# Narrower stationary operands and a reordered chunk loop in an RWKV-7 kernel with a gated projection

## The chip, the cores and the metric

The kernel runs on one core of one Trainium2 chip. The metric is the device time of one execution in microseconds (us), and a kernel's time is the median of several executions. Nearly all runs of this study fell in the fast state (on one core this only means that a run did not stand over 1.5% above the fastest of its kernel). The exceptions are two of the four runs of e6_shift and six of the 113 runs of before that were made beside the experiments. Ratios use fast runs alone. Every run's output matched the reference.

Five engines work side by side (in before's profile the busy shares of four of them, 86, 58, 42 and 22%, add up to more than the span): TensorE (matmuls are "PE" in the profile, loads of the stationary operand "PEld"), VectorE (DVE), ScalarE (ACT), GpSimd (POOL) and SyncE (SP). "PEclk" is what the profile gives as the share of the full clock that was granted to TensorE.

## The reference

```python
# r, k, v, w, a, b: [4 batches, 8 heads, 768 steps, 40]
for t in range(S):                       # state: [4, 8, 40, 40]
    y[:, :, t] = einsum('bhd,bhde->bhe', r_t, state)
    Sa = einsum('bhde,bhe->bhd', state, a_t)
    state = state * w_t - einsum('bhd,bhe->bhde', Sa, b_t) \
          + einsum('bhd,bhe->bhde', v_t, k_t)
x = y as (3072, 320)                     # the bridge
h = x @ w_in                             # (3072, 2048)
out = (h * cos(h)) @ w_out               # (3072, 320)
```

## The kernel before

The recurrence is solved in 24 chunks of 32 steps. Each chunk is a list of *pieces* of TensorE work, with their evictions. The narrow pieces belong to the recurrence. Their operands occupy only 32 to 64 rows and columns, and several matmuls run on the array at a time: in before's trace eight of x start per 62.5 ns, about what 72 columns alone take at the 216 ns for 256 columns of a wide piece. Between them stand transposes. The wide pieces, `M` in the lists below, are a quarter of a step of the two dense products `x @ w_in` and `(h cos h) @ w_out` for tokens that are already done. They fill the time in which the recurrence waits for evictions.

| name in the list | tile in the profile | what it does | TensorE records |
|---|---|---|---|
| t | sT | state transposed | 16 |
| q | qps | r times state | 128 |
| x | x0ps | right-hand side of the triangular system | 256 |
| s | sps | its solution | 128 |
| z | dps | state update and output | 256 |
| g | gram | products of k, a, v, r of the next chunk | 256 |
| v, k, pw, pa, pb | vT, kT, wT, wn, bT | transposes | 8 to 16 |
| pn | nps | matrix for the inverse | 256 |
| M | ph or po | one quarter of a dense product | 16, some 32 |

A *record* is a load or a matmul as the trace has it. Each fp32 `matmul` call leaves two of both, so the 64 calls of z are 128 loads and 128 matmuls.

```python
    def ch_q(c):
        ps = at("qps")
        for i in range(2 * B):
            for e in range(2):
                for f in range(2):
                    mm(ps[full[e], f, i * C : (i + 1) * C], G["s"][half[f], i, full[e]],   # 64 columns
                       G["rT", c][half[f], 2 * (i % 2) + e, blk[i // 2]], i == 0)
        nc.scalar.copy(...)                       # one eviction of 128 rows into qz
    ...
    def first_b(g, j):
        first_full(g, j, 1)                       # 8 matmuls of 128 rows
        ...                                       # then the tails: 8 matmuls of 64 rows
    ...
        for c in range(NCH):
            ...
            elif c % 4 == 0 and q0 < NCH:
                segs = [t, M, v, q, M, k, x, M, g, M, s, M, pb, z, M, pn, M, M]
            elif c % 4 == 1 and q0 < NCH:
                segs = [t, M, v, q, M, k, x, M, pw, M, s, g, M, z, M, pa, M, pa1, M]
            elif c % 4 == 2 and q0 < NCH:
                segs = [t, M, pb, q, M, pn, M, x, v, M, s, k, M, z, M, g, M, M]
            elif c % 4 == 3 and q0 + 4 < NCH:
                segs = [t, M, pw, q, M, v, x, M, k, M, s, g, M, z, M, pa, M, pa1, M]
            else:
                segs = [t, M, v, M, q, M, k, x, M, g, M, s, M, z, M, M]
```

(Laid out more tightly than in the source, and cut. In most chunks a wide piece stands between two long narrow ones. That turns out to matter.)

## Time and profile before

| | before |
|---|---|
| median device time, first three runs | 875.13 us (872.48 to 877.44) |
| profiled execution | 869.9 us, mean granted clock 0.929 |
| TensorE matmuls / loads busy | 86% / 67% |
| VectorE / ScalarE busy | 58% / 42% |

The prediction below shows and reads the main lines. One line of the same page it does not show, and did not look at: among the DMA queues stands `q8 instruction: 130, 2.13, 1.0%`. These are 130 packets of 2.13 MB together, so 16,384 bytes each, that took 1.0% of the span of 16 DMA engines. By the profile's name for it the queue delivers instructions, not data. With its small share of the DMA engines' time it looks harmless.

### The profile page before, as it was taken

How to read it: one execution, taken by the hardware profiler on the slowest of the kernel's cores; microseconds unless marked ns; L12 is line 12 of the kernel's file. 1: busy time of each engine (PE TensorE's matmuls, PEld its weight loads, DVE VectorE, ACT ScalarE, POOL GpSimd, SP SyncE). 2: the span in 40 equal slices, each digit the busy share in tenths (PEclk: the TensorE clock that was granted, in tenths of full speed). 3: DMA queues.
4: the chain of work that ended last, by engine and by line, in shares of the span. 5: the costliest groups of instructions: out<-in, count | busy, mean ns of one | idle time of the engine just before them, and what ended most of it. 6: DMA issues, size and time to landing. Idle time of an engine off the chain costs nothing.

```text
span 869.9 us, 36861 instructions
## 1 busy us (share of the span) xinstructions
PE 751.9 (86%) x16472; PEld 585.0 (67%) x16472; DVE 505.5 (58%) x1074; ACT 364.5 (42%) x683; POOL 195.6 (22%) x342
## 2 busy tenths in 40 slices
PE   3535463998888997989999999999999999999997
PEld 3423352676666775777777777777777777777775
DVE  7788787349635597425578435588335775323322
ACT  0316555333234432534443453444435443534343
POOL 4306534120202132012132013203102221111000
PEclk9855567898999999999999999999999999999999
DMA  7456352412140420430420422313312202201000
GB/s 97 108 91 190 109 157 57 78 27 42 32 72 17 73 58 10 71 66 12 74 62 24 71 54 41 72 35 57 69 23 41 55 20 44 41 20 35 19 15 16
DMA packets 181854, 49.07 MB, mean 56 GB/s; under 512 B 156992, under 2 KB 178496, under 8 KB 181696
## 3 DMA queue, kind: packets, MB, share of 16 engines
q1 hardware_dynamic: 179264, 46.05, 25.4%
q8 instruction: 130, 2.13, 1.0%
q10 hardware_dynamic: 2176, 0.33, 0.3%
q0 software_dynamic: 256, 0.33, 0.2%
q14 instruction: 28, 0.23, 0.1%
HBM read 38.80 MB, written 7.86 MB: 54 GB/s over the span
## 4 chain that ended last, share of the span: by engine, by line
PE 63%; DVE 22%; ACT 7%; issue 4%; DMA 2%; POOL 0%; SPq 0%; DVEq 0%; ACTq 0%
PE ph L101 24%; PE po L101 17%; DVE inv L409 4%; PE dps L101 4%; DVE inv_tmp L405 4%; PE x0ps L101 3%; PE qps L101 2%; DVE rw L352 2%; PE gram L101 2%; PE sT L495 2%; DVE turns L649 2%; DVE wb L331 2%; PE nps L101 1%; ACT turns L654 1%; PE sps L101 1%
## 5 line engine op out<-in xcount | busy, mean ns | idle before, releaser
L101 PE MATMUL po<-w_out_sb,gT 128*128 128x320 f32 x768 | 228.2, 444 | 0.0
L101 PE MATMUL ph<-xT,w_in_sb 128*128 128x256 f32 x768 | 195.4, 401 | 11.0 <-DVE gT L657 8.0
L101 PEld LDWEIGHTS po<-w_out_sb,gT 128*128 128x128 f32 x768 | 141.4, 193 | 54.3 <-issue 4.8
L101 PEld LDWEIGHTS ph<-xT,w_in_sb 128*128 128x128 f32 x768 | 145.3, 198 | 33.9 <-issue 11.6
L649 DVE SCALAR_TENSOR_TENSOR turns<-turns,ph 128x512 f32<-128x512 f32 x96 | 61.7, 684 | 149.9 <-ACT turns L647 149.9
L647 ACT ACTIVATE turns<-ph,rnd 128x512 f32<-128x512 f32 x96 | 60.8, 684 | 199.6 <-PE ph L101 199.6
L586 POOL TENSOR_TENSOR qz<-qz,wc 128x160 f32<-128x160 f32 x92 | 42.8, 483 | 268.2 <-DVE qz L585 267.6
L657 DVE TENSOR_TENSOR gT<-ph,turns 128x512 f32<-128x512 f32 x96 | 65.4, 686 | 39.8 <-ACT turns L654 39.6
L409 DVE TENSOR_TENSOR inv<-inv,inv_tmp 128x31 f32<-128x31 f32 (+15 forms) x186 | 68.4, 368 | 6.4
L654 ACT ACTIVATE turns<-turns,half_pi 128x512 f32<-128x512 f32 x96 | 69.4, 722 | 3.1
L405 DVE TENSOR_TENSOR inv_tmp<-u,inv 128x31 f32<-128x31 f32 (+15 forms) x186 | 67.4, 362 | 4.2
L653 ACT ACTIVATE turns<-turns 128x512 f32<-128x512 f32 x96 | 60.3, 628 | 17.2 <-DVE turns L649 17.2
L585 DVE TENSOR_TENSOR qz<-dps,qz 128x160 f32<-128x160 f32 x92 | 29.2, 318 | 50.7 <-PE dps L101 50.7
L101 PE MATMUL ph<-xT,w_in_tail 64*128 64x256 f32 x384 | 54.4, 402 | 0.0
L352 DVE RECIPROCAL rw<-wn 128x320 f32<-128x320 f32 x24 | 51.6, 2151 | 3.3 <-PE wn L290 3.0
L101 PEld LDWEIGHTS ph<-xT,w_in_tail 64*128 64x128 f32 x384 | 33.1, 186 | 18.1 <-issue 15.7
L101 PE MATMUL dps<-vvm,kn 32*64 32x72 f32 x1536 | 28.5, 248 | 18.9 <-DVE sm L558 8.8
L101 PEld LDWEIGHTS dps<-vvm,kn 32*64 32x64 f32 x1536 | 22.7, 139 | 28.8 <-issue 15.1
L499 ACT COPY s<-sT 128x512 f32<-128x512 f32 x46 | 24.5, 585 | 36.3 <-PE sT L495 36.3
L333 POOL COPY wc<-wb 128x16 f32<-128x16 f32 x24 | 5.7, 237 | 137.6 <-DVE wb L331 137.6
L597 POOL TENSOR_TENSOR yt<-yt,wb 128x512 f32<-128x512 f32 x24 | 31.6, 1315 | 22.1 <-DVE yt L592 22.1
L536 DVE COPY x<-x0ps 128x288 f32<-128x288 f32 x24 | 10.8, 452 | 43.0 <-ACT x L535 43.0
(108 smaller groups left out, 1040.6 us busy)
## 6 DMA issues: line engine op xcount, KB each, us to landing
words<-in_moe_w_in_dram SPq DMA_DIRECT2D x8, 512.0 KB
nat_k<-in_k_dram SPq DMA_DIRECT2D x96, 40.0 KB
nat_v<-in_v_dram SPq DMA_DIRECT2D x96, 40.0 KB
nat_r<-in_r_dram SPq DMA_DIRECT2D x96, 40.0 KB
xd<-yt SPq DMA_DIRECT2D x48, 80.0 KB
out_dram<-ot SPq DMA_DIRECT2D x24, 160.0 KB
nat_w<-in_w_dram SPq DMA_DIRECT2D x88, 40.0 KB
nat_b<-in_b_dram SPq DMA_DIRECT2D x88, 40.0 KB
```

Of the source, the lines that this page charges most:

```text
L101: nc.tensor.matmul(o, lhsT=lhsT, rhs=rhs, start=start, stop=stop, skip_group_check=True)
L352: nc.vector.reciprocal(rw, unpad(wn.rearrange("p (h d) -> p h d", h=H)))
L405: nc.vector.tensor_tensor(tmp, u[:, j : j + 1, :j].to_broadcast([P, C - j, j]), x[:, j:, j : j + 1].to_broadcast([P, C - j, j]), ALU.mult,)
L409: nc.vector.tensor_tensor(x[:, j:, :j], x[:, j:, :j], tmp, ALU.subtract)
L585: nc.vector.tensor_tensor(z, pick(dp, 0, (2 * N72 + C, 2), (N72, 2), (1, D)), z, ALU.add)
L586: nc.gpsimd.tensor_tensor(z, z, wc.rearrange("p (f m b) -> p f m b", f=2, m=2)[:, :, :, bb] .unsqueeze(3).to_broadcast([P, 2, 2, D]), ALU. ...
L597: nc.gpsimd.tensor_tensor(yt.rearrange("p j b t -> p (j b) t"), yt.rearrange("p j b t -> p (j b) t"), wx, ALU.mult)
L647: nc.scalar.activation(n, u, ACTF.Identity, bias=rnd, scale=1.0)
L649: nc.vector.scalar_tensor_tensor(n, n, -ROUND, u, ALU.add, ALU.subtract)
L653: nc.scalar.activation(n, n, ACTF.Abs)
L654: nc.scalar.activation(n, n, ACTF.Sin, bias=half_pi, scale=-2.0 * math.pi)
L657: nc.vector.tensor_tensor(gT[:, 2 * e : 2 * e + 2].rearrange("p f t -> p (f t)"), us[e], ns[e], ALU.mult)
```

## The change

The intent is to spend less TensorE time on loads and on changes of the array's shape:

1. q, and the half of z that uses `bn`, load only the 40 columns that carry data, in place of 64. The price is a second eviction for q.
2. Pieces of one array shape are put next to each other: gram (g) directly behind x, and in every fourth chunk x directly behind pn, with x's state part first.
3. The 64-row "tails" of the first dense product come first when the piece ahead of them was narrow, so that the array goes from narrow to 64 rows to 128 rows.

```diff
-                        ps[full[e], f, i * C : (i + 1) * C], G["s"][half[f], i, full[e]],
+                        ps[half[e], f, i * C : (i + 1) * C], G["s"][half[f], i, half[e]],
 ...
+        for rows in half:
+            nc.scalar.copy(pick(qz[rows], ...), ps[rows, ...])
 ...                                             # ch_z, bn half
-                            n[blk[bb], 2 * j + e, :],
+                            n[blk[bb], 2 * j + e, : rows[e].stop - rows[e].start],
 ...                                             # first_b
+        if G["small"]:
+            tails(True)
+            first_full(g, j, 1, False)
+        else:
+            first_full(g, j, 1)
+            tails(False)
 ...                                             # c % 4 == 0, 1, 2, 3, and the last chunks
-                segs = [t, M, v, q, M, k, x, M, g, M, s, M, pb, z, M, pn, M, M]
+                segs = [t, M, v, q, M, k, x, g, M, s, M, pb, M, z, M, pn, M, M]
-                segs = [t, M, v, q, M, k, x, M, pw, M, s, g, M, z, M, pa, M, pa1, M]
+                segs = [t, M, v, q, M, k, x, g, M, pw, M, s, M, z, M, pa, M, pa1, M]
-                segs = [t, M, pb, q, M, pn, M, x, v, M, s, k, M, z, M, g, M, M]
+                segs = [t, M, pb, q, M, pn, x, M, v, M, s, k, M, z, M, g, M, M]
-                segs = [t, M, pw, q, M, v, x, M, k, M, s, g, M, z, M, pa, M, pa1, M]
+                segs = [t, M, pw, q, M, v, M, k, x, g, M, s, M, z, M, pa, M, pa1, M]
-                segs = [t, M, v, M, q, M, k, x, M, g, M, s, M, z, M, M]
+                segs = [t, M, v, q, M, k, x, g, M, s, M, M, z, M, M, M]
```

(Cut: the plumbing of `small` and of x's two parts, and c=4, which changes in the same way.)

More of the change, by code (lines that the diff above doesn't have):

```diff
@@ L304, in later, with step @@
         waiting.append([steps, work])
-    def step(work, of_inv=0, of_w=0):
+    def step(work, of_inv=0, of_w=0, small=False):
         before = list(waiting)
         work()
+        G["small"] = small
         for w in before:
@@ L506, in ch_q, with ch_x, of_a, of_state @@
                     mm(
-                        ps[full[e], f, i * C : (i + 1) * C], G["s"][half[f], i, full[e]],
+                        ps[half[e], f, i * C : (i + 1) * C], G["s"][half[f], i, half[e]],
                         G["rT", c][half[f], 2 * (i % 2) + e, blk[i // 2]], i == 0,
                     )
-        nc.scalar.copy(
-            pick(qz, 0, (NZ - C, 2), (NZ, 2 * B), (1, C)),
-            ps[:, :, : 2 * B * C].rearrange("p f (i t) -> p f i t", t=C),
-        )
-    def ch_x(c):
-        ps = at("x0ps")
-        for j in range(4):
-            o = C * (j // 2)
-            for bb in range(B):
-                for e in range(2):
-                    mm(
-                        ps[blk[bb ^ e], e, j * N72 : (j + 1) * N72], G["ag", c][blk[bb], 4 * e + j, :],
-                        vvm[c % 2][blk[bb], 2 * j + e, o : o + N72], j == 0,
-                    )
-        if c:
+        for rows in half:
+            nc.scalar.copy(
+                pick(qz[rows], 0, (NZ - C, 2), (NZ, 2 * B), (1, C)),
+                ps[rows, :, : 2 * B * C].rearrange("p f (i t) -> p f i t", t=C),
+            )
+    def ch_x(c, state_first=False):
+        ps = at("x0ps")
+        def of_a(first):
+            for j in range(4):
+                o = C * (j // 2)
+                for bb in range(B):
+                    for e in range(2):
+                        mm(
+                            ps[blk[bb ^ e], e, j * N72 : (j + 1) * N72],
+                            G["ag", c][blk[bb], 4 * e + j, :],
+                            vvm[c % 2][blk[bb], 2 * j + e, o : o + N72], first and j == 0,
+                        )
+        def of_state(first):
             for j in range(4):
@@ L531, in ch_x @@
                             ps[blk[bb ^ e], e, j * N72 : (j + 1) * N72],
-                            G["aT", c][half[e], j, blk[bb]], qz[half[e], bb, j % 2, o : o + N72], False,
-                        )
+                            G["aT", c][half[e], j, blk[bb]],
+                            qz[half[e], bb, j % 2, o : o + N72], first and j == 0,
+                        )
+        parts = [of_a] if c == 0 else [of_state, of_a] if state_first else [of_a, of_state]
+        for i, part in enumerate(parts):
+            part(i == 0)
         x0 = [sb1.tile([P, 4 * N72], F32, tag=f"x0{e}", name=f"x0{e}") for e in range(2)]
@@ L568, in ch_z @@
         for s, n in ((0, kn_b[c % 2]), (1, bn_b[c % 7])):
+            rows = half if s else full
             for j in range(4):
@@ L573, in ch_z @@
                         mm(
-                            ps[bb // 2][full[e], bb % 2, j * N72 : (j + 1) * N72],
-                            n[blk[bb], 2 * j + e, :],
+                            ps[bb // 2][rows[e], bb % 2, j * N72 : (j + 1) * N72],
+                            n[blk[bb], 2 * j + e, : rows[e].stop - rows[e].start],
                             sm[e][blk[bb], j, :] if s else vvm[c % 2][blk[bb], 2 * j + e, o : o + N72],
@@ L628, in first_a, with first_full @@
         first_full(g, j, 0)
-    def first_full(g, j, e):
+    def first_full(g, j, e, fresh=True):
         xT, ph = G["xT", g], G["ph"][e]
@@ L634, in first_full, with tails @@
                 cs = slice((4 * j + 2 * e + f) * P, (4 * j + 2 * e + f + 1) * P)
-                mm(ph[:, f, :], w_in_sb[:, i, cs], xT[:, i, :], i == 0 and f == 0, False)
+                mm(ph[:, f, :], w_in_sb[:, i, cs], xT[:, i, :], fresh and i == 0 and f == 0, False)
     def first_b(g, j):
-        first_full(g, j, 1)
         xT, phs = G["xT", g], G["ph"]
-        for f in range(2):
-            for e in range(2):
-                mm(phs[e][:, f, :], w_in_tail[full[e], j, f, :], xT[full[e], 2, :], False)
+        def tails(fresh):
+            for f in range(2):
+                for e in range(2):
+                    mm(
+                        phs[e][:, f, :], w_in_tail[full[e], j, f, :], xT[full[e], 2, :],
+                        fresh and e == 1 and f == 0, False,
+                    )
+        if G["small"]:
[4 more added lines that the diff above has]
+            tails(False)
         us = [ph.rearrange("p f t -> p (f t)") for ph in phs]
@@ L726, in last @@
                 later(1, lambda: p2_kn(c + 2))
-        return [lambda: ch_t(c), lambda: ch_q(c), lambda: ch_x(c), lambda: ch_s(c), last]
+        return [lambda: ch_t(c), lambda: ch_q(c), lambda: ch_x(c, c == 5 or c > 5 and c % 4 == 2), lambda: ch_s(c), last]
     with tc.manual_schedule():
@@ L814 @@
                 pw, pa, pa1, *p8 = p1(8)
-                segs = [t, M, v, q, M, k, x, M, g, M, s, M, z, M, pw, M, pa, pa1, M]
+                segs = [t, M, v, q, M, k, x, g, M, s, M, M, z, M, pw, M, pa, pa1, M]
                 fill = (3, 0)
@@ L849 @@
                 if seg is not M:
-                    step(seg, *fill)
+                    step(seg, *fill, small=seg in (q, x, g, s, z, pn))
                 elif empty > 0:
```

## The prediction

> **What bounds the kernel now.** I first read the page: busy shares, the 40 slices and the chain that ended last.
>
> ```profile
> PE 751.9 (86%) x16472; PEld 585.0 (67%) x16472; DVE 505.5 (58%) x1074; ACT 364.5 (42%) x683; POOL 195.6 (22%) x342
> ...
> PE   3535463998888997989999999999999999999997
> DVE  7788787349635597425578435588335775323322
> ...
> PEclk9855567898999999999999999999999999999999
> ...
> PE 63%; DVE 22%; ACT 7%; issue 4%; DMA 2%; POOL 0%; SPq 0%; DVEq 0%; ACTq 0%
> ```
>
> Up to about 225 us, and again from 313 to 338 us, the chain runs through VectorE (inv, inv_tmp: the triangular inverse). From chunk c=8 (352 us) to the end TensorE is nearly always busy at full clock, so a TensorE nanosecond saved there is one off the span. "Busy" is no measure of useful streaming, though. So I next read the timeline of TensorE for one stretch (c=13) and took the differences of the start times, first column:
>
> ```profile
> 511.35 1.14 PE L101 MATMUL qps<-rT,s 40*64 40x32 f32 x64
> 512.41 1.99 PE L101 MATMUL ph<-xT,w_in_sb 128*128 128x256 f32 x8
> 514.33 1.13 PE L101 MATMUL ph<-xT,w_in_tail 64*128 64x256 f32 x8
> 515.40 0.66 PE L290 MATMUL kT<-ident,kn 128*128 128x128 f32 x4
> 515.99 0.88 PE L101 MATMUL x0ps<-vvm,ag 32*32 32x72 f32 x64
> 516.80 0.89 PE L101 MATMUL x0ps<-qz,aT 40*32 40x72 f32 x64
> 517.61 2.42 PE L101 MATMUL po<-w_out_sb,gT 128*128 128x320 f32 x8
> 519.87 1.04 PE L290 MATMUL wT<-ident,nat_w 128*128 128x128 f32 x8
> ```
>
> Here q takes 1.06 us, the full products of the second half 1.92, the tails 1.07, kT 0.59, x 1.62 (two parts), po 2.26. Where the shape before and after is the same, the same work is shorter: eight full ph records take 1.73 us (216 ns each, as at 508.65), eight po 2.16, four transposes 0.44. Thus each change of array shape costs two things. The last record of the old shape stands 93 ns longer (309 ns to the next start in place of 216; 203 in place of 109 after transposes). And the first load of the new shape lies bare: po 2.26 less 2.16 is 0.10 us, about as much for ph and tail, 0.055 for a transpose, and I take 0.055 for a 64-column and 0.03 for a 32-column load.
>
> Inside q, starts of single records come in fours (the four 64x64 tiles), a period of 58 ns. Loads of one tile lie 55 ns apart at the start; streaming 32 columns twice takes only 27 ns (at 216 ns for 256 columns). So q waits for its loads. In z the same 64-column load hides: its period is 62.5 ns for eight tiles, just the 72 columns, and later in the stream 66 ns for eight, whatever the load's width (x and nps with 32 columns do the same).
>
> [...]
>
> **The change part by part.**
>
> *q, 40 columns.* [...] The period becomes about 38, and sixteen periods save 16 x 20 = 0.31 us with the ends. All 23 q calls get it, but only those outside the VectorE-bound stretches count: c=5, 6, 8 to 23, 18 calls, 18 x 0.31 = 5.6 us. The price is a second eviction of q: the row of qz<-qps shows 586 ns per copy of 128 rows; I assume that one of 40 rows takes as long, as the columns are the same, so ACT gets 23 x 0.59 = 13.5 us more. ACT is 42% busy and x comes 3 us later; I put nothing.
>
> *z, 40 columns for bn.* That load is hidden by streaming and by issue, so little: 0.5 us in all.
>
> *Fewer shape changes.* I wrote down the order of pieces per chunk before and after, by the loop's own rules. Tails first after a narrow piece: "q, full, tail, full" becomes "q, tail, full", one change fewer, 0.15 to 0.2 us. Gram directly behind x: x's second part and gram have both 40 rows and 32 columns, so "x, po, gram" loses two changes, 0.2 + 0.12 = 0.32 us. For c mod 4 = 2, x behind pn with the state part first saves the change between them. Counting all: 340 changes become 291, with 2 or 3 fewer per chunk, and 7.1 us for c from 4 on; without c=4 and 7, where VectorE rules, 6.7 us.
>
> *Waits that go.* For c = 8, 12, 16 z follows bT and waits for its eviction, as both PSUM buffers of the pool are needed. The chain of waits at c=12:
>
> ```profile
> 495.56 0.89 PE bT L290 x8
> 496.45 0.02 issue
> 496.48 1.08 ACT bT L366 x2
> 497.56 0.04 issue
> 497.60 1.63 PE dps L101 x87
> ```
>
> The changed order puts a product between: 3 x 1.1 = 3.3 us. For c = 9, 11, 13, 15, 17, 19 gram stands one product before z and its buffer is still being read by VectorE: z takes 1.77, 2.09, 2.09, 2.40, 2.06, 2.13 in place of 1.57, together 3.1 us; the new order frees it earlier. Likewise s to gram at c = 9, 13, 17 (waiting for the scan of pw), 0.27 each, 0.8.
>
> *A wait that comes.* Gram needs the eviction of kT. With k, x, gram in a row, only x (1.5 us) hides it. At c=13 the ACT timeline shows how late kT is:
>
> ```profile
> 515.50 1.27 ACT L647 ACTIVATE turns<-ph,rnd 128x512 f32<-128x512 f32 x2 [2.37 <-PE ph L101]
> 516.94 0.63 ACT L653 ACTIVATE turns<-turns 128x512 f32<-128x512 f32 x1 [0.18 <-DVE turns L649]
> 517.60 0.72 ACT L654 ACTIVATE turns<-turns,half_pi 128x512 f32<-128x512 f32 x1
> 518.23 0.57 ACT L458 COPY kT<-kT 128x512 f32<-128x512 f32 x1
> ```
>
> The products end at 515.40, kT is out at 518.80, 3.4 us later. Tails first complete the first half's PSUM 1.8 us earlier, so one rounding (0.68) moves out of this row and VectorE's part is done in time: kT at 2.7 us. TensorE arrives at 0.53 + 1.53 = 2.06. So gram waits about 0.66 us where k follows the products directly, c = 8, 9, 12, 13, 16, 17: 4.0 us lost. In the other chunks another product lies between. At c=19 "v, q, k" without a product costs about 1 us for buffers.
>
> Sum: 5.6 + 0.5 + 6.7 + 3.3 + 3.1 + 0.8 - 4.0 - 1.0 = 15.0 us. 875.1 - 15.0 = 860.
>
> **The rivals.** (a) Loads and streams of one tile run one after the other, not side by side: 27 + 27 + gaps also gives 58 ns. Then 40 columns save 10, not 20 ns, q gives 2.8 us, and the time is 863. Against it: nps (32-column loads, 32-column streams) starts in periods of 28 to 32 ns, which leaves no room for both in turn. (b) The kT wait is worse: if the rounding does not move forward (a wait on all of TensorE's earlier work, not on the first half), each wait is 1.3 us, -4 more, 864; with gram's arrival delaying x0 and s behind it, 867. For it: the ACT timeline above, where kT stands behind all of that row. (c) The kernel's rhythm is set by VectorE/ACT in more chunks than I think, so saved TensorE time comes back as waits: then half of 15, 867. Against it: from 414 to 690 us VectorE is busy 164 of 275 us, and TensorE 269. (d) Better: c=4 to 7, where TensorE idles some 15 us, gains from the new order too, and kT does not wait; 853.
>
> **How the range follows.** The counted parts (q, changes) are well founded; 12 us. The waits, +7 and -5, are each uncertain by half. TensorE also has stalls with no visible cause, 1.2 to 2.2 us each, about five after 250 us, which can move by some us, and the runs before spread by 5 us. So 853 to 868. Two per cent is 857.6, a little under my centre: faster 0.37, same 0.60, slower 0.03.
>
> **What would show it.** q's load row at 40 columns and q's start-to-next-start 0.75 us (0.90 if rival a). Gram behind x without the 93 ns step; tails 64*128 directly behind qps and dps. Chunks of about 30.5 us near 29. A wait gram <- ACT kT of about 4 us after 352 us (8 with rival b), and the waits dps <- ACT bT and dps <- DVE vvm gone. Wrong if q stays above 1 us, if shape changes cost the same after the reorder [...], or if new waits on ACT exceed 8 us.

The period of 38 ns for q is the prediction's estimate. It can be had from the trace of before, where the first two loads of one tile start 55 ns apart at 64 columns (q) and 108 at 128 (tails): 40/64 of 55 is 34 ns, 21 less, and 58 - 21 is 37. The 0.03 us that it takes for a 32-column load are, in the same way, half of the 55 ns. The 27 ns for streaming are 32/256 of the 216 that a record of 256 columns takes; that a load takes 27 ns too is rival (a)'s assumption.

## The result, and the profile after

The changed kernel took **913.48 us** (median of 4 runs, 909.94 to 916.62). The kernel before took 876.29 us (872.48 to 878.26, 4 runs) beside it. The ratio is 1.0429, 95% interval 1.0374 to 1.0483: slower, and far outside the predicted range of 853 to 868. A ratio in this document is the mean time of one kernel's fast runs over the mean time of the other's in the same rounds, so it is not quite the ratio of the medians quoted.

From the page of the changed kernel come the busy shares, the slices of TensorE and of its clock, the instruction queue, and the chain that ended last:

```profile
PE 762.4 (84%) x16472; PEld 591.3 (65%) x16472; DVE 508.0 (56%) x1074; ACT 378.2 (42%) x706; POOL 196.4 (22%) x342
...
PE   4525464888978879899999899989999899989997
...
PEclk9755576999989889999999989989999999999999
...
q8 instruction: 130, 2.13, 1.0%
...
PE 66%; DVE 17%; ACT 7%; issue 7%; DMA 2%; SPq 0%; POOL 0%; ACTq 0%; DVEq 0%
```

The work is the same, 16,472 matmuls, and yet their busy time grew from 751.9 to 762.4 us, although q's loads became narrower. "issue", time in which TensorE waits for nothing that the profile knows, went from 4 to 7% of the span. In the clock's row new dips to 8 stand in the middle, where before every slice from the eleventh on showed a 9.

The windows from c=8 to the end, first of before, then of after, put a size on it (columns: window, its length, busy us and count of PE, PEld, DVE, ACT, POOL, then granted clock, DMA share, GB/s):

```profile
352.40:864.30 511.90, 503.21 (x10764) 390.61 (x10763) 259.13 (x575) 226.89 (x425) 92.80 (x168) 1.00 0.21 43
```

```profile
361.80:905.40 543.60, 512.15 (x10765) 396.26 (x10763) 261.17 (x575) 236.56 (x441) 93.66 (x168) 0.96 0.21 40
```

This stretch became 31.7 us longer. TensorE's idle time in it (length less PE busy) rose from 8.7 to 31.5 us, and the clock fell from 1.00 to 0.96. No other engine has noticeably more to do, except the 16 more q copies of ACT, and in after all of them are less than half busy.

The view of waits, of the same stretch, for TensorE's loads, names what the loads waited for (us in total, times, longest); before, then after:

```profile
PEld gram L101 <- issue: 6.2, 15, 1.4
PEld dps L101 <- ACT bT L366: 3.1, 3, 1.0
...
PEld po L101 <- issue: 2.0, 6, 0.3
```

```profile
PEld gram L101 <- issue: 19.0, 14, 2.4
PEld po L101 <- issue: 13.7, 41, 2.3
...
PEld gram L101 <- ACT kT L459: 4.3, 8, 0.7
```

The wait for bT went, as predicted, and the wait for kT came, at its predicted size. But gram's waits for "issue" tripled, and single ones are 2.4 us long. So the timeline of TensorE for c=13, the same stretch as the prediction shows of before (columns: start, length, engine, line, out<-in, shape, elements, count, and in brackets the idle time ahead):

```profile
531.44 0.81 PE L101 MATMUL qps<-rT,s 40*40 40x32 f32 x64
532.18 1.13 PE L101 MATMUL ph<-xT,w_in_tail 64*128 64x256 f32 x8
533.25 1.99 PE L101 MATMUL ph<-xT,w_in_sb 128*128 128x256 f32 x8
535.08 0.60 PE L290 MATMUL kT<-ident,kn 128*128 128x128 f32 x4
535.61 0.88 PE L101 MATMUL x0ps<-vvm,ag 32*32 32x72 f32 x64
536.42 0.88 PE L101 MATMUL x0ps<-qz,aT 40*32 40x72 f32 x64
537.77 0.72 PE L101 MATMUL gram<-aT,kT 40*32 40x32 f32 x61 [0.46 <-ACT kT L459]
...
538.33 0.73 PE L101 MATMUL gram<-rT,vT 40*32 40x32 f32 x62
540.50 3.63 PE L101 MATMUL po<-w_out_sb,gT 128*128 128x320 f32 x8 [1.44 <-issue]
543.97 0.71 PE L290 MATMUL wT<-ident,nat_w 128*128 128x128 f32 x5
```

Differences of the first column: q 0.74 us, tails 1.07, the full products behind them 1.83. All these are gains, of the sizes predicted. Then two new things. Behind gram TensorE stops: po starts 2.17 us after gram's second half did, where 62 such records take 0.7 us, and the profile names no releaser. And po then takes 3.47 us in place of 2.26, since the trace's clock records show half clock from 539.78 to 543.19 us, a stretch of 3.41.

### What the stops have in common

I next listed, from the trace, the gaps between TensorE records (from the start of one to the start of the next), with the number of records executed by then, and the packets of the instruction queue. This number counts, besides loads and matmuls, the semaphore instructions of TensorE's sequencer, which the profile's pages leave out (344, and 3 drains, in after): without them the regularity below does not show, so I take it that they are fetched too. Six of after's gaps, and three of before's:

```text
start us  gap us  records/256  between                    packet start+us  restart after landing
after
 252.62    2.30      30.75     x0ps -> x0ps               252.4+1.24        1.29
 404.49    1.72      53.75     gram -> gram               403.6+1.24        1.36
 436.65    1.96      58.75     x0ps -> x0ps               436.3+1.07        1.21
 538.98    1.51      75.75     po load -> po matmul       537.9+1.02        1.55
 606.89    2.13      86.75     gram -> gram               606.4+1.33        1.30
 814.76    2.49     122.75     gram -> gram               814.7+1.35        1.24
before
 253.06    2.41      30.75     x0ps -> x0ps               252.6+1.32        1.54
 439.45    1.48      61.75     gram -> gram               438.6+0.93        1.43
 371.91    1.10      48.81     dps -> dps (wait for bT)   366.5+1.00        5.50
```

A gap with a known releaser, the last row, stands at another count (48.81 here, and 70.64 and 92.46 where before waits for bT again). The others in the list, which the profile calls "issue", all stand where the number of records is a whole number and three quarters of 256, and end 1.2 to 1.6 us after a packet of the instruction queue has landed. (Not every "issue" is of this kind: a few of 0.5 to 1.3 us stand elsewhere, such as one of 1.14 us at 28.08 in after, 2.5 us after a landing.) After's 33,291 records are 130.04 times 256, for 130 packets; a packet of 16,384 bytes for 256 records is 64 bytes a record. I read this so: TensorE gets its instructions in blocks of 256, and at these points it had run out of them. In the rows above that cost 1.5 to 2.5 us each time.

A block's supply can be worked out (an estimate from the traces). Where blocks follow each other as fast as they can, in e7_run further down, a packet starts 1.0 to 1.2 us after TensorE has entered a block, takes 0.9 to 1.4 us, and TensorE goes on 1.3 to 1.6 us later, together some 3.6 us in the middle of these ranges (3.75 by the period). In after the start of the packet varies more: the blocks ahead of its 24 stalls take 2.2 to 5.4 us from their first record to the restart, with a median of 3.6. Why, I did not find. A block lasts by its content: x, z and gram are 256 records each, and take about 1.6, 1.5 and 1.2 us. If a block lies wholly in narrow pieces, TensorE stands still for the rest, about 2 us. If one wide piece of 16 records lies in it, the block takes 240/256 of 1.5 us and another 1.8 to 2.3 us, 3.2 to 3.7 us, and the fetch is just about hidden. Before, a wide piece stood between x and gram. The change put x and gram next to each other, 512 narrow records, and 512 records in a row always hold a whole block. The same goes for pn and x.

### The account of the profiles

For each profiled execution, from 240 us to the end, I added up the gaps of over 0.5 us that stand at a block's count and end 1.1 to 1.65 us after a landing ("fetch stalls"), and the time at half clock (without a stretch that runs into the kernel's end). The last column is an estimate: half of the throttled time in which TensorE was not idle.

| kernel | fetch stalls | their sum, us | at half clock, us | cost of half clock, us |
|---|---|---|---|---|
| before | 4 | 7.1 | 6.8 | 3.3 |
| after | 24 | 41.5 | 64.9 | 27.9 |
| e1_q40 | 8 | 11.1 | 10.2 | 4.5 |
| e2_z40 | 8 | 10.4 | 13.7 | 6.7 |
| e3_tails | 8 | 11.9 | 13.7 | 6.8 |
| e4_order | 19 | 30.0 | 54.6 | 24.6 |
| e5_no_order | 10 | 12.8 | 20.5 | 8.9 |
| e6_shift | 18 | 30.5 | 30.7 | 12.1 |
| e8_spread | 9 | 9.4 | 13.7 | 6.8 |
| e9_pn_x | 14 | 17.5 | 27.3 | 12.8 |
| e10_x_g | 12 | 16.2 | 23.9 | 11.7 |
| e11_spread_shift | 7 | 9.7 | 17.1 | 7.2 |

After less before: stalls 34.4 and half clock 24.6, 59.0 us. The spans differ by 911.0 - 869.9 = 41.1. So something gave 17.9 us back, and the gains that the prediction had added up are 15.0. These are single profiles: e2_z40, whose edit changes next to nothing, has 4 stalls more than before and a time no different from it, so a difference of a few stalls shows nothing by itself.

### The profile page after: what moved, and what is told of

Its sections match the earlier page's. It is cut to its first block, busy times and chain, and to the rows that moved or that the text cites. A ratio compares the mean times of both kernels' runs of the same rounds, so it can differ in the third digit from the quotient of the medians.

```text
span 911.0 us, 36920 instructions
## 1 busy us (share of the span) xinstructions
PE 762.4 (84%) x16472; PEld 591.3 (65%) x16472; DVE 508.0 (56%) x1074; ACT 378.2 (42%) x706; POOL 196.4 (22%) x342
## 3 DMA queue, kind: packets, MB, share of 16 engines
q8 instruction: 130, 2.13, 1.0%
## 4 chain that ended last, share of the span: by engine, by line
PE 66%; DVE 17%; ACT 7%; issue 7%; DMA 2%; SPq 0%; POOL 0%; ACTq 0%; DVEq 0%
PE ph L101 23%; PE po L101 21%; PE dps L101 4%; DVE inv L410 4%; DVE inv_tmp L406 3%; PE gram L101 3%; PE sps L101 2%; PE x0ps L101 2%; PE nps L101 2%; DVE wb L332 2%; DVE rw L353 2%; PE sT L496 2%; PE qps L101 1%; ACT turns L679 1%; PE bT L290 1%
## 5 line engine op out<-in xcount | busy, mean ns | idle before, releaser
L101 PE MATMUL po<-w_out_sb,gT 128*128 128x320 f32 x768 | 238.3, 459 | 1.4 <-issue 1.4
L101 PE MATMUL ph<-xT,w_in_sb 128*128 128x256 f32 x768 | 200.0, 408 | 8.3 <-DVE gT L682 8.0
L101 PEld LDWEIGHTS po<-w_out_sb,gT 128*128 128x128 f32 x768 | 147.2, 199 | 63.2 <-issue 16.2
L101 PEld LDWEIGHTS ph<-xT,w_in_sb 128*128 128x128 f32 x768 | 149.2, 202 | 43.1 <-issue 21.1
L672 ACT ACTIVATE turns<-ph,rnd 128x512 f32<-128x512 f32 x96 | 64.3, 687 | 172.9 <-PE ph L101 172.6
L101 PE MATMUL ph<-xT,w_in_tail 64*128 64x256 f32 x384 | 59.1, 429 | 0.0
L500 ACT COPY s<-sT 128x512 f32<-128x512 f32 x46 | 24.6, 586 | 44.6 <-PE sT L496 44.5
L101 PEld LDWEIGHTS ph<-xT,w_in_tail 64*128 64x128 f32 x384 | 35.6, 200 | 10.2 <-issue 5.2
L101 PE MATMUL x0ps<-vvm,ag 32*32 32x72 f32 x1536 | 23.7, 240 | 20.7 <-issue 8.8
L101 PE MATMUL gram<-rT,vT 40*32 40x32 f32 x1536 | 21.6, 210 | 22.6 <-issue 22.6
L484 ACT COPY vvm<-gram 128x256 f32<-128x256 f32 x24 | 8.9, 371 | 71.5 <-DVE ag L479 71.5
L569 DVE TENSOR_TENSOR sm<-sps,su 128x128 f32<-128x128 f32 x48 | 11.7, 286 | 45.9 <-ACT sm L564 45.9
```

The source lines that it names most:

```text
L101: nc.tensor.matmul(o, lhsT=lhsT, rhs=rhs, start=start, stop=stop, skip_group_check=True)
L500: nc.scalar.copy(G["s"][:, 4 * i : 4 * i + 4].rearrange("p i e -> p (i e)"), ps[:, i])
L672: nc.scalar.activation(n, u, ACTF.Identity, bias=rnd, scale=1.0)
```

## The experiments

The theory **F** (fetch): the loss comes from the order alone, because joined narrow pieces outrun the supply of instructions; the half clock follows from that. Rivals: the narrower operands or the second q copy bring it, by a new rhythm of ACT; **C**, particular neighbours are slow, whatever the count of records; **D**, narrow products issue at their usual rate however many follow each other, and the stalls are accidents of this program. The diffs are against before or after, as said. The three calls to the chip had their own runs of before: medians 873.0 (31 runs), 870.7 (43) and 870.22 us (39).

### e4_order: the order alone

Before, with after's lists of pieces and x's state part first in the same chunks, but 64 columns and tails last.

```diff
-                segs = [t, M, v, M, q, M, k, x, M, g, M, s, M, z, M, M]
+                segs = [t, M, v, q, M, k, x, g, M, s, M, M, z, M, M, M]
 ...                                             # and the other lists as in the change
```

> The changed order of pieces alone (gram directly behind x, state part first behind pn), q and z at 64 columns, tails where they were. Theory F: all of the loss and more, as the gains of q and of the tails are missing: 920 us (910 to 930), some 20 stalls of 1 to 2.4 us, each at a record count of 192 modulo 256, and over 50 us of half clock after 240 us. Rival A: close to the kernel before, 865 to 880. Rival B (the wait of gram for the eviction of kT): slow too, but its idle time ends with ACT kT and is 1.3 us or more in each chunk that has k, x, gram in a row, 8, 9, 12, 13, 16, 17.

Measured: 913.73 us (910.65 to 918.49, 4 runs), ratio 1.0481 (1.043 to 1.0532), slower. The order alone carries the whole loss, and the rival of operands and copies falls. The run also answers a smaller question: with tails last, gram waits 1.39 us for kT (x takes 2.86 us), with tails first 0.68. So the prediction's account of kT's way through ACT was right in both of its cases.

### e5_no_order: all but the order

After, with before's lists.

```diff
-                segs = [t, M, v, q, M, k, x, g, M, s, M, M, z, M, M, M]
+                segs = [t, M, v, M, q, M, k, x, M, g, M, s, M, z, M, M]
 ...                                             # the other lists too
```

> The change without its new order: q and half of z at 40 columns and the tails placed by their neighbours, on the order of before. Theory F: 867 us (862 to 872): q 5.6, z 0.8, fewer shape changes 2.7 us off; few stalls (up to 6), throttled time under 15 us after 240 us. Rival A: about as slow as the whole change, 900 or more. Rival B: faster too, so this run does not part F from B.

Measured: 869.15 us (864.41 to 873.14, 20 runs), ratio 0.9965 (0.9945 to 0.9985): a real gain, a small one. It is within what was expected, but its 10 fetch stalls (12.8 us) and 20.5 us of half clock are more than the 6 and 15 us forecast. That part of what the quicker pieces gain is lost again to the fetch is likely, but not shown: e2_z40 and e3_tails have 8 stalls as well.

### e1_q40, e2_z40, e3_tails: the other parts one by one

```diff
 # e1_q40, on before
-                        ps[full[e], f, i * C : (i + 1) * C], G["s"][half[f], i, full[e]],
+                        ps[half[e], f, i * C : (i + 1) * C], G["s"][half[f], i, half[e]],
+        for rows in half: nc.scalar.copy(...)
 # e2_z40, on before
-                            n[blk[bb], 2 * j + e, :],
+                            n[blk[bb], 2 * j + e, : rows[e].stop - rows[e].start],
 # e3_tails, on before: only "if G["small"]: tails first"
```

> The kernel before, with only q at 40 columns and its eviction in two copies. Theory F (instruction fetch): the loss of the change comes from long runs of narrow products that outrun the fetch of TensorE's instructions, 256 at a time, and not from the 40 columns; so this run is faster by 18 x 0.31 us, about 870.5 us (867 to 874), q takes 0.75 us in place of 1.06, and there are no more than some 6 unexplained stalls of over 0.5 us after 240 us. Rival A (the doubled eviction on ScalarE delays the rest): 890 us or more, with new waits on ACT.

> Only the second half of z at 40 columns: its loads are hidden, z goes from 1.57 to 1.53 us, 20 x 0.04 = 0.8 us, which the spread covers: 872.5 us (868 to 877). If z were bound by its loads it would fall by up to 0.3 us a call and the kernel by 6 us.

> The tails placed by their neighbours alone, on the order of before with 64 columns: 18 changes of shape fewer by the count of the pieces, 2.7 us: 870.5 us (866 to 875). A single changed piece, T of a tails-first product, still takes 1.06 us, and the full products behind it 1.83 in place of 1.92.

Measured: e1_q40 873.45 us (869.87 to 878.76, 12 runs), ratio 1.0003 (0.9979 to 1.0026); e2_z40 871.7 us (865.76 to 876.26, 20 runs), 0.9994 (0.997 to 1.0018); e3_tails 868.42 us (864.01 to 873.12, 20 runs), 0.9977 (0.9956 to 0.9998). The tails' 0.2% is near what was expected. The miss is e1: q takes 0.75 us in every chunk in place of 1.06, and yet the time did not move. In its profile there are 8 fetch stalls, more than the 6 forecast and than before's 4. That they ate the gain is not shown, as e2_z40 and e3_tails have 8 as well. By the chunks' starts in the two profiles, the stretch from c=8 to the end did become shorter, 514.2 us in place of 517.5, so 3.3 of the 5.0 us counted for its 16 q; but c=8 began 2.8 us later. Where stalls fall, and when c=8 begins, varies between executions by such amounts (349.4 to 355.2 us in the profiles of before, e1, e2, e3 and e5), so the cause of this miss stays open.

### e6_shift: the same program, 64 transposes later

If a stall belongs to a place in the program (C), nothing moves when work is put ahead of everything. If it belongs to a count of records, every stall moves to another instruction.

```diff
+        shift = at("shift")
+        for i in range(64):
+            nc.tensor.transpose(shift[:, (i // 4) % 2, (i % 4) * P : (i % 4 + 1) * P], ident, ident)
         first, other = p1(0), p1(2)
```

> The whole change, with 64 more transposes of the identity (128 TensorE records, 7 us at most, in the start where TensorE waits for loads) ahead of everything. Theory F: the stalls still come at a record count of 192 modulo 256, but as the program is shifted by half a block against the count, other pieces hold them: where the changed kernel stalls at the end of gram's second product it now stalls inside x or the middle of gram, and so on; time 905 to 925 us. Rival C (joining x and gram, or pn and x, in one array shape is slow as such): the stalls stay at the same places of the program and the count at them moves by 128.

Measured: 890.16 and 902.56 us; two more runs, 903.89 and 906.34, stand over 1.5% above the quickest and count as slow. The ratio of the two fast ones is 1.0264 (1.0166 to 1.0362): slower than before by the mean, unclear by the 2% rule. Three of the four times lie below what was expected, and the profiled run is the quickest. The timeline of TensorE at c=13:

```profile
518.83 0.72 PE L101 MATMUL gram<-aT,kT 40*32 40x32 f32 x62 [0.46 <-ACT kT L459]
...
520.78 0.74 PE L101 MATMUL gram<-rT,vT 40*32 40x32 f32 x63 [1.19 <-issue]
521.45 2.42 PE L101 MATMUL po<-w_out_sb,gT 128*128 128x320 f32 x8
```

In after TensorE stopped behind gram's last record, here it stops between gram's two halves, 128 records earlier, which is what 64 transposes put ahead. The count at the stop is the same in both, 75.75 blocks. All 18 fetch stalls of this profile stand at three quarters of a block, 14 of them at a count at which after stalls too, though the shift puts other instructions there. C falls.

### e7_run: narrow products alone

To measure the supply by itself, 512 narrow calls (2,048 records, eight blocks) that depend on nothing new stand behind everything else of before. Their result is not used.

```diff
+        run = at("run")
+        for i in range(64):
+            for bb in range(B):
+                for e in range(2):
+                    mm(run[blk[bb ^ e], e, :N72], su[blk[bb], 0, :], vvm[0][blk[bb], e, :N72], True)
```

> The kernel before with one uninterrupted run of 512 narrow products (1024 loads and 1024 matmuls by the trace's count, 8 blocks of 256) at its very end, where no other engine works and no product waits for data. Theory F: the run goes at one block in about 3.6 us, the period of the fetches, so the kernel is 26 to 30 us longer (about 902 us), the run shows stalls of about 2 us at a distance of 256 records, each ending 1.2 to 1.6 us after a fetch has landed. Rival D (TensorE issues narrow products at 8.3 ns a pair, as within a stream, and the stalls came of something between the pieces): 1024 x 8.3 ns = 8.5 us longer, about 882 us, and no stalls.

Measured: 895.81 us (891.3 and 900.32), 25.1 us over before, just under the 26 to 30 expected, ratio 1.0282 (1.0216 to 1.0349). The timeline at the end:

```profile
874.18 1.75 PE L101 MATMUL run<-vvm,su 32*32 32x72 f32 x128 [1.97 <-issue]
878.20 2.22 PE L101 MATMUL run<-vvm,su 32*32 32x72 f32 x128 [2.27 <-issue]
881.95 2.22 PE L101 MATMUL run<-vvm,su 32*32 32x72 f32 x128 [1.53 <-issue]
885.42 2.22 PE L101 MATMUL run<-vvm,su 32*32 32x72 f32 x128 [1.25 <-issue]
```

Each row is one block, 128 matmuls with their loads, and a stop ahead of each. From 874.18 to 896.65, where the last one starts, are six blocks, 3.75 us per block, and the packets of the instruction queue start at the same distance (3.5 to 4.1 us). The 8.3 ns of rival D are the pace in the middle of a stream (66 ns for eight, in the prediction's reading of before); the run's first 236 pairs, ahead of its first stop, took 2.53 us, 10.7 ns each, which would make the run 11 us long. It took 25, so D falls. From 875.33 us, 5.9 us into it, the run also went at half clock, though TensorE never stopped for more than 2.6 us in it. That makes the rows 2.22 us long, but does not explain the period: at half clock the 128 starts of a row span 1.9 us, and eight such blocks would be 15 us.

### e8_spread: keep the parts that gain, spread the narrow pieces

If F holds, the order should do the opposite: a wide piece between any two of pn, x, g, s and z where one is to be had. e8_spread is e5 with four lists changed. They also take the waits of before that the prediction had found (z behind bT's and gram's evictions).

```diff
 # on e5_no_order: c % 4 == 0, 1, 3, and c == 5
-                segs = [t, M, v, q, M, k, x, M, g, M, s, M, pb, z, M, pn, M, M]
+                segs = [t, M, v, q, M, k, x, M, g, M, s, pb, M, z, M, pn, M, M]
-                segs = [t, M, v, q, M, k, x, M, pw, M, s, g, M, z, M, pa, M, pa1, M]
+                segs = [t, M, v, q, M, k, x, M, pw, g, M, s, M, z, M, pa, M, pa1, M]
-                segs = [t, M, pw, q, M, v, x, M, k, M, s, g, M, z, M, pa, M, pa1, M]
+                segs = [t, M, pw, q, M, v, x, M, k, M, g, s, M, z, M, pa, M, pa1, M]
-                segs = [t, M, pb, q, M, pn, x, M, v, pw, M, k, M, s, g, M, z, M, pa, pa1, M]
+                segs = [t, M, pb, q, M, pn, M, x, v, pw, M, k, M, s, g, M, z, M, pa, pa1, M]
```

> An attempt at a version that beats both: q and half of z at 40 columns, tails by neighbours, on the order of before, with the narrow pieces kept apart: bT ahead of the product before z (c mod 4 = 0), pw and gram between two products (c mod 4 = 1), gram ahead of s (c mod 4 = 3), and a product between pn and x at c = 5. Theory F: the waits of z for evictions go (3.3 + 2.3 + 0.9 us) and the two stalls at c = 5 (3.5 us): 861 us (855 to 868). If the fetch takes back what the waits give, as it did in e5: 866 to 871.

Measured: 858.32 us (853.28 to 859.48, 6 runs), ratio 0.9842 (0.9805 to 0.9879). It beats both kernels: 1.6% under before, too little for "faster" by the 2% rule. From its page, the busy shares and the clock:

```profile
PE 743.4 (87%) x16472; PEld 578.7 (68%) x16472; DVE 506.7 (59%) x1074; ACT 377.7 (44%) x706; POOL 196.0 (23%) x342
...
PEclk9755557899999998999999999999999999999999
```

TensorE is busy 743.4 us for the same 16,472 matmuls, 19.0 less than in after. z takes 1.53 us at c=9, 12 and 13, so the waits ahead of it are gone; at c=8 it still takes 2.13 and at c=15 2.43. It has no fewer fetch stalls than before (9 against 4). So what it gains over before is not the supply of instructions but those waits and the quicker q, z and tails; what it shows of F is that these gains can be had where the joins are left out.

### e9_pn_x and e10_x_g: put one join back

e8_spread is a good ground for the reverse test, as it has few stalls of its own. e9_pn_x joins pn and x in five chunks, e10_x_g x and gram in the last four that have a gram (its list also moves two other products of these chunks).

```diff
 # e9_pn_x, on e8_spread (c % 4 == 2, and c == 5 alike; x's state part first)
-                segs = [t, M, pb, q, M, pn, M, x, v, M, s, k, M, z, M, g, M, M]
+                segs = [t, M, pb, q, M, pn, x, M, v, M, s, k, M, z, M, g, M, M]
 # e10_x_g, on e8_spread
-                segs = [t, M, v, M, q, M, k, x, M, g, M, s, M, z, M, M]
+                segs = [t, M, v, q, M, k, x, g, M, s, M, M, z, M, M, M]
```

> e8_spread with one of the change's two joins put back: x directly behind pn, state part first, at c = 5, 6, 10, 14, 18. A run of 512 narrow records holds a whole block of 256 wherever the boundaries fall. Theory F: one stall of about 2.1 us inside x or pn at each of the five, 10.5 us, some of them followed by a window of 3.41 us at half clock (up to 1.7 us each), less five times 0.27 us for the shape change saved: 870 us (865 to 876). If the joined shape were a gain as I predicted: 857.

> e8_spread with the other join put back, in the last kind of chunk alone (c = 19 to 22; there k has no wait for its eviction, as the changed kernel's trace shows): gram directly behind x. Theory F: four stalls of about 2.2 us in gram, and 3 or 4 half-clock windows of 1.7 us, less 4 x 0.32: 869 us (864 to 874). If the joined shape were a gain: 857.

Measured: e9_pn_x 874.49 us (869.05 to 882.03, 20 runs), ratio to before 1.0049 (1.0026 to 1.0073); e10_x_g 871.12 us (863.67 to 875.95, 20 runs), 0.9992 (0.9968 to 1.0016). Beside e8_spread's 858.32 us of the call before, whose before was within half a microsecond of this one's, that is 16 us lost by five joins and 13 by four: some 3 us a join, though each saves a change of the array's shape. (e8_spread ran on another chip; e11_spread_shift, below, ran in this call, at 855.6.) In e10's profile all four joins stall, in gram, for 2.02, 1.97, 2.10 and 2.58 us from start to start. The first of them in the timeline:

```profile
680.87 0.70 PE L101 MATMUL gram<-aT,kT 40*32 40x32 f32 x51
683.38 0.28 PE L101 MATMUL gram<-aT,kT 40*32 40x32 f32 x6 [1.82 <-issue]
```

In e9's four of five do, in x (2.03, 2.36, 1.53, 2.51 us). The fifth, c=18, has only about 0.5 us; why, I did not find.

### e11_spread_shift: e8 with the 64 transposes of e6

> e8_spread with the same 64 transposes ahead as e6 (128 records, in the time in which TensorE waits for loads). Theory F: where the boundaries of the blocks fall decides which narrow pieces fill a block, so the stalls move; with no run over 384 records they stay few (4 to 12), and the time within 858 +- 8 us.

```diff
+        shift = at("shift")                      # e8_spread, with e6's 64 transposes ahead of all
```

Measured: 855.6 us (851.94 to 858.41, 4 runs), ratio 0.9833 (0.9782 to 0.9885), unclear by the 2% rule and not to be told from e8_spread. It has 7 stalls, 9.7 us, at other instructions than e8's, all but one in s and z around c=7, 11 and 15. So e8's gain is no luck of the count. What moves by the count is only which of the remaining stalls occur.

## Why the prediction was wrong

**The step that failed: "Fewer shape changes".** The prediction wrote "340 changes become 291" and took them at some 0.15 us each, 6.7 us in all. The saving itself is there: where nothing is waited for (c = 19 to 21 of after), gram starts 1.42 to 1.44 us after x, without a step between them, and in before the next piece starts 1.62 us after x. But the term counted the joining of narrow pieces as pure gain. It left out what the wide piece between them does: its 16 records last as long as 256 narrow ones and more (1.8 to 2.3 us, x 1.6), and give the next block of instructions time to arrive. In place of the gain (some 4 of the 6.7 us; the other 2.7 are those of the tails, and e3_tails has them nearly) the new order cost 913.73 - 873.0 = 40.7 us (e4_order, the order alone). That is a balance: the waits that went are already counted in it, and so are the waits for kT, 8.5 us there in the view of waits.

**The observation that was at hand.** The prediction noted "stalls with no visible cause, 1.2 to 2.2 us each, about five after 250 us, which can move by some us", and put them into the range as noise. They were the mechanism. In before's trace they stand at counts 30.75, 32.75, 49.75 and 61.75. An unexplained wait of 2 us in front of a chain of independent matmuls deserved the question of what it has in common with the others; the page's instruction queue would have answered it. None of the four rivals named the supply of instructions, so the range could not hold the result.

**"A TensorE nanosecond saved there is one off the span"** was not borne out either. In e1_q40 18 x 0.31 us of TensorE time were saved, as counted, and the median stayed (ratio 0.9979 to 1.0026), though in the profile 3.3 us came off from c=8 on. That saved TensorE time becomes a stall where a block lasts only about as long as its successor's fetch is argued, and no run shows it for q.

**Half clock was not foreseen.** The prediction read "at full clock" off before's page and kept it for after. The 14 stretches at half clock in after's trace after 240 us (without the one at the kernel's end) last 3.41 or 6.83 us; 13 begin within about 4 us of the start of a fetch stall, and one behind gram's wait at c=7, for kT's eviction. That the stalls bring them on is read from this coincidence, and from before and e8 having few of both; no run separates the two. The stretches of the clock's records in after are multiples of 3.41 us (3.41, 6.83, 10.24 and so on, but for the one at the end). In the 3.41 us ahead of each of the 14 TensorE was idle for 1.0 to 2.7 us only, and worked in the rest. Cut into windows in step with the stretches, after's trace from 240 us on has eight windows at full clock with over 1.75 us idle, each followed by half clock; of the eleven with 0.97 to 1.75 us, six are, and of those with less, none. So what goes with half clock in this trace is idle time, of whatever cause, within a window.

**What was right.**

- *q, 40 columns.* 0.75 us from start to start in place of 1.06, just the 0.31 predicted. In the traces at c=13 the loads of one tile start 35 ns apart in place of 55, and the period is 38.4 ns in place of 58. So q was bound by its loads and rival (a) is refuted. The second copy takes 581 ns at 40 rows, as assumed, and ACT's 364.5 us of work became 378.2, without harm.
- *z, 40 columns.* 1.57 became 1.53 us, near nothing, as said. e2_z40 shows no change of time.
- *Tails first.* Tails 1.06 us and full products 1.83, as counted; e3_tails gains 0.23%, 2.0 us of 870.7.
- *The waits that go.* The waits of dps for bT and for gram's eviction are gone from after's view of waits, and from e8_spread's.
- *The wait that comes.* Gram's wait for kT, predicted at 0.66 us each and 4.0 in all, makes it 2.16 us from x to gram in place of the 1.42 to 1.44 without a wait, so some 0.7, at c = 8, 9, 12, 13, 16 and 17 as predicted; the view of waits has 4.3 us. Rival (b) is refuted, as rounding does move forward with tails first.
- *c=7 bound by VectorE.* It still is: gram waited 3.2 us there before, and 5.3 after.

Rival (c), a rhythm set by VectorE and ACT, does not explain it: from c=8 on neither engine is busy for half of after's time, and the waits that grew are those for "issue". Rival (d), in which c = 4 to 7 gain too, fell: they took 155.7 us in place of 145.4 in the profiles.

**What stays open.** Why the stalls' counts stand at three quarters of a block and not at a whole one; instructions that leave no record would do it, but that is only argued. How many blocks can wait ahead of TensorE: the four joins of e10_x_g, 512 narrow records each, stalled once each, and no run measured more. How much of the half clock would remain without the stalls. How the first chunks share in the loss: from c=8 on the window became 31.7 us longer, so 9.4 us of the 41.1 came earlier, where VectorE sets the time in part. By the chunks' starts most of it is c=6, 38.3 us in place of 29.6: in it after has two fetch stalls (2.1 and 2.3 us) and 10.2 us of half clock, and before neither. How much of it they caused is not split.

## What to carry to other kernels

Look for TensorE gaps without a releaser, and count the records between them, loads and TensorE's semaphore instructions included: if they stand a whole number of blocks of 256 apart, and each ends soon after a packet of the instruction queue has landed, the supply of instructions is the likely bound, as it was in this case. By the traces of this kernel (3.75 us a block in e7_run), let no 256 TensorE records in a row last less than about 3.7 us; put a wide product between small ones, even where a change of the array's shape could be saved by joining them. A change that shortens narrow pieces, such as q's here, may then pay less than it saves (e1_q40: nothing of 5.6 us, for a reason that is not shown).
